# A written-out order of work with 73 places moved, and the last gate and value weights in one transfer each, in a kernel of two attentions and a gated feed-forward layer

## The chip, the cores and the metric

The kernel runs on one core of one Trainium2 chip. A core has a matrix engine (TensorE, in profiles PE; its weight loads are shown apart as PEld), a vector engine (VectorE, DVE), a scalar engine (ScalarE, ACT), a general engine (GpSimd, POOL) and a sync engine (SyncE, SP) which here only issues transfers. Each works through its own list of instructions in order and waits at semaphores for the others. Transfers between device memory (DRAM) and the core's SBUF run on 16 DMA engines beside them; PSUM is the small memory into which the matrix engine writes, eight banks of it.

The metric is the device time of one execution in microseconds (us).

## The reference, cut to what matters

Two attentions are computed per head and added: one over the sequence pooled by four, and one in which a position sees only the positions less than four away. The sum, with the heads laid side by side, goes through a feed-forward layer with a gate.

```python
batch, n_heads, seq, head_dim = (8, 8, 576, 64)
n_tokens, d_model, d_ff = (4608, 512, 1536)

def _attn_ref(q, k, v):                      # factor = 4, Sd = 144
    q_d = q.reshape(B, H, Sd, factor, D).mean(axis=3)     # k_d, v_d likewise
    out_d = sm_attn(q_d, k_d, v_d)
    out_up = np.repeat(out_d, factor, axis=2)
    mask = np.abs(pos[:, None] - pos[None, :]) < factor
    scores = np.where(mask, scale * np.matmul(q, k.transpose(0, 1, 3, 2)), -1e9)
    ...
    return out_up + np.matmul(attn, v)

def _moe_ref(x, w_gate, w_val, w_out):
    gate = np.maximum(x @ w_gate, 0.0)
    val = x @ w_val
    return gate * val @ w_out
```

## The kernel before

**The attention** goes by pairs of heads, 32 of them, numbered p = 0 to 31; four pairs make one batch of 576 tokens. Each pair is a chain of named steps, and the pair's number ends the name:

- lq, lk (L1430) load q and k; from pair 4 on one transfer serves two pairs. cast (L1330) turns them to 16 bits. For pairs 0 to 3 the loads land in the still unused tile gT and the casts in the still unused tile wo_sb, which is why these names stand in the trace.
- T (L1456, and L1460 for pairs 0 to 3) transposes them on TensorE into PSUM, for pairs 0 to 7; from pair 8 on a transposing transfer dT does it. ev0 and ev1 (one ev from pair 8 on) copy the result to qkT, pl pools it into qkd (L1330 for pairs 0 to 3, L1507 afterwards).
- S (L1518 the band, L1530 the pooled part; in pairs 0 to 3 two steps Sl, with the mask at L1537, and Sd) makes the scores in PSUM.
- msk, mx, sub, exp, sm, rc, nrm are the softmax of the band; nrm (L1615) multiplies by the reciprocal; tr0 and tr1 (L1621) transpose on VectorE.
- dmx, nb, exd0 to exd2 (L1605), rcd, nrd (L1631) are the softmax of the pooled scores. W (L1640) transposes them on TensorE and evw copies them out, for pairs 0 to 7; from pair 8 on a transfer dW does it.
- lv0 to lv3 (L1680) load v, vc (L1330) casts it. VP (L1695) and vd pool it (from pair 12 on l4, vs and vd).
- V (L1731, L1739) multiplies with v; od (L1750) scales the pooled part; xa0 and xa1 (L1759) add the two and write xT, the input of the feed-forward layer.

**The feed-forward layer** goes by blocks of tokens: 512 and 64 for the first batch and the second, then 512. For each of the 12 slices of d_ff (number j), hg and hv (L1798) multiply a block with a slice of the gate weights wg_sb and the value weights wv_sb, rl (L1812) is the ReLU and gm (L1819) the product into gT. hg0_6 is block 0, slice 6. hg512 and hg1088 are the small blocks of 64 tokens, six slices each. In the first block the slices 0 and 1 are split: hg0_0a works on three of the four parts of d_model, hg0_0b on the last, which comes from pair 3. y (L1864) multiplies 128 tokens of gT with wo_sb, yc (L1873) copies the result out and st stores it.

**The weights** come by transfers that GpSimd issues. The gate and value weights wg_sb and wv_sb come in four pieces each, 384 columns (three slices) a piece: wg0 to wg3 and wv0 to wv3, all at L1380; the output weights in four pieces wo0 to wo3 at L1385.

**What sets the order.** Every step is an Op with its engine (or several that could do it), its length as the author puts it, what it depends on, and a priority. A function list_schedule plans them all, with a model of the five engines, the transfers and the fetching of TensorE's instructions, and the result is one list of steps. A table RANKS of some 300 entries shifts priorities by name. The steps are then emitted in that order, and so each engine's list, the choice among engines, and the PSUM banks are fixed. Where the planner sees TensorE wait in the first 34 us of its plan, it fills the gap with matmuls of zeros (emit_zeros, L1360), 41 in all beside 12 at the very start (pewarm). Below, "a fill" is one such matmul.

Steps wait for one another by semaphores which the framework sets from the tiles that they read and write; SP's transfers also wait, each for the one eight places ahead of it.

## Time and profile before

| | us |
|---|---|
| median of 3 runs | 362.52 |
| lowest, highest | 361.52, 364.54 |
| the profiled execution, whole | 364.42 |
| its span, first to last instruction | 362.6 |
| busy: TensorE | 351.6 |
| busy: VectorE | 248.0 |
| busy: GpSimd | 204.7 |
| busy: ScalarE | 203.2 |

The span is what the views of the trace show; 1.8 us of the profiled execution's time lie around it. The mean granted clock of TensorE was 0.999.

How to read the rows: a row of the timeline has the start, the time, the engine, the line and operation, the tile written and those read, the size, how many alike were merged (x), and in square brackets how long the engine was idle before it and what released it. SPq is SP's queue of transfers. A row of windows has the stretch, its length, and for each engine the busy time and the count of instructions.

### The profile page before, as it was taken

Reading aid. Unit: us, or ns where it says so; the run is one execution under the profiler, and the core shown is the slowest. Engines: PE = TensorE matmul, PEld = TensorE weight load, DVE = VectorE, ACT = ScalarE, POOL = GpSimd, SP = SyncE. Lnnn points to the kernel's source line nnn. Section 1 sums busy time; section 2 is a strip of 40 time slices with the busy share of each in tenths; the row PEclk is TensorE's granted clock in tenths of the full one; section 3 lists DMA queues with packets and bytes.
Section 4 is the critical chain, followed back from the end, with each engine's and each line's share of the span. In section 5 each row is a group of like instructions: output and inputs, shape, how many; then the busy total and the mean of one; then the engine's idle time right before and its main releaser. Section 6 shows DMA issues by size and latency. Waiting matters only on the chain.

```text
span 362.6 us, 10503 instructions
## 1 busy us (share of the span) xinstructions
PE 351.6 (97%) x4241; PEld 182.4 (50%) x4241; DVE 248.0 (68%) x477; ACT 203.2 (56%) x481; POOL 204.7 (56%) x240
## 2 busy tenths in 40 slices
PE   8988998999999999999999999999999999999996
PEld 3545555445545554545545445444545454445554
DVE  4667997717988798978875986788979854222210
ACT  2477785627874857664566584767565533233222
POOL 7798573942477988674877468485899400000000
PEclk9999999999999999999999999999999999999999
DMA  7999999789999999999999999999996121011012
GB/s 185 190 260 258 195 188 302 124 181 165 283 225 215 219 275 167 254 225 250 196 220 243 164 303 156 215 282 174 238 236 101 40 77 47 0 60 59 0 72 105
DMA packets 122067, 64.80 MB, mean 179 GB/s; under 512 B 100386, under 2 KB 106402, under 8 KB 122018
## 3 DMA queue, kind: packets, MB, share of 16 engines
q1 hardware_dynamic: 116194, 59.41, 77.3%
q0 software_dynamic: 5824, 4.72, 8.5%
q8 instruction: 33, 0.54, 0.7%
q14 instruction: 16, 0.13, 0.1%
HBM read 47.59 MB, written 9.44 MB: 157 GB/s over the span
## 4 chain that ended last, share of the span: by engine, by line
PE 71%; DMA 13%; POOL 4%; SPq 4%; DVE 3%; issue 3%; ACT 1%; POOLq 0%; DVEq 0%; ACTq 0%
PE bank L1798 42%; PE bank L1864 20%; DMA qk<-in_q_dram 3%; DMA tq<-c 3%; PE bank L1518 2%; DMA v<-in_v_dram 2%; DMA vw<-in_v_dram 2%; PE bank L1731 2%; POOL wd L1631 1%; DMA gT<-in_q_dram 1%; SPq L1430 1%; PE bank L1739 1%; DMA wT<-wd 1%; PE bank L1530 1%; DVE qkd L1507 1%
## 5 line engine op out<-in xcount | busy, mean ns | idle before, releaser
L1819 DVE TENSOR_TENSOR gT<-r,bank 128x512 f16<-128x512 f16 (+1 forms) x112 | 74.5, 666 | 62.5 <-PE bank L1798 59.2
L1798 PE MATMUL bank<-xT,wg_sb 128*128 128x512 f16 (+2 forms) x528 | 112.3, 341 | 0.0
L1798 PE MATMUL bank<-xT,wv_sb 128*128 128x512 f16 (+2 forms) x528 | 112.2, 341 | 0.0
L1812 ACT ACTIVATE r<-bank 128x512 f16<-128x512 f32 (+1 forms) x112 | 65.1, 582 | 67.6 <-PE bank L1798 63.2
L1864 PE MATMUL bank<-wo_sb,gT 128*128 128x512 f16 x420 | 96.7, 379 | 0.0
L1798 PEld LDWEIGHTS <-wg_sb 128*128 128x128 f16 x528 | 44.2, 98 | 45.5 <-issue 0.4
L1798 PEld LDWEIGHTS <-wv_sb 128*128 128x128 f16 x528 | 44.2, 98 | 44.7 <-issue 0.9
L1864 PEld LDWEIGHTS <-gT 128*128 128x128 f16 x420 | 39.8, 98 | 44.6 <-issue 0.4
L1873 ACT COPY y_sb<-bank 128x512 f32<-128x512 f32 x35 | 20.5, 585 | 50.5 <-PE bank L1864 48.0
L1330 POOL CAST vw<-vw 128x1536 f16<-128x1536 f32 x28 | 40.9, 1462 | 3.4 <-DMA vw<-in_v_dram 2.5
L1507 DVE TENSOR_REDUCE qkd<-qkT 128x288 f16<-128x1152 f16 x28 | 37.6, 1342 | 4.9 <-ACT qkT L1329 4.4
L1586 POOL TENSOR_TENSOR s_sb<-s_sb,mx 128x384 f32<-128x384 f32 x28 | 23.2, 831 | 27.8 <-DVE mx L1583 27.1
L1605 ACT ACTIVATE wd<-bank,nmb 128x144 f16<-128x144 f32 x96 | 35.6, 380 | 5.0 <-POOL nmb L1595 4.2
L1621 DVE STREAM_TRANSPOSE at<-e 64x384 f16<-64x384 f16 x64 | 36.4, 569 | 2.0 <-POOL e L1615 1.3
L1615 POOL TENSOR_TENSOR e<-e,rs 128x384 f16<-128x384 f16 x32 | 26.8, 840 | 14.4 <-DVE rs L1613 10.8
L1631 POOL TENSOR_TENSOR wd<-wd,rsd 128x432 f16<-128x432 f16 x32 | 29.0, 909 | 9.6 <-DVE rsd L1627 8.3
L1759 DVE TENSOR_TENSOR xT<-bank,od_sb 128x288 f16<-128x288 f32 (+2 forms) x68 | 26.7, 430 | 9.5 <-ACT od_sb L1750 9.4
L1329 ACT COPY qkT<-tq 128x1152 f16<-128x1152 f16 x21 | 25.3, 1205 | 3.8 <-DMA tq<-c 3.8
L1717 POOL TENSOR_TENSOR vs<-v 104x512 f32<-104x512 f32 x20 | 25.4, 1269 | 1.4 <-DMA v<-in_v_dram 1.1
L1518 PEld LDWEIGHTS <-qkT 64*32 64x32 f16 x1536 | 16.6, 90 | 11.8 <-issue 7.2
L1330 POOL CAST c<-qk 128x1152 f16<-128x1152 f32 x16 | 18.2, 1147 | 5.7 <-issue 3.3
L1518 PE MATMUL bank<-qkT 64*32 64x32 f16 x1536 | 20.2, 178 | 0.9 <-DVE xT L1759 0.7
(67 smaller groups left out, 357.6 us busy)
## 6 DMA issues: line engine op xcount, KB each, us to landing
vw<-in_v_dram SPq DMA_DIRECT2D x126, 96.0 KB, 4.8
out_dram<-y_sb SPq DMA_DIRECT2D x16, 512.0 KB, 4.2
qk<-in_q_dram SPq DMA_DIRECT2D x14, 576.0 KB, 7.1
qk<-in_k_dram SPq DMA_DIRECT2D x14, 576.0 KB, 6.9
v<-in_v_dram SPq DMA_DIRECT2D x10, 640.0 KB, 7.1
wv_sb<-in_moe_w_val_dram POOLq DMA_DIRECT2D x4, 384.0 KB, 10.3
wg_sb<-in_moe_w_gate_dram POOLq DMA_DIRECT2D x4, 384.0 KB, 10.0
wo_sb<-in_moe_w_out_dram POOLq DMA_DIRECT2D x4, 384.0 KB, 7.8
```

Source lines behind the costliest of these rows:

```text
L1330: return lambda o: engine[eng].tensor_copy(out=dst, in_=src(o))
L1507: nc.vector.tensor_reduce(out=qkd[S3].rearrange("p (x t) -> p x t", x=2), in_=qk_sums, axis=AX.X, op=ALU.add)
L1518: nc.tensor.matmul(out=scv[32 * c : 32 * c + 32, i, :], lhsT=cols(hh, q0 + step * 24 * blk, 32), rhs=cols(hh, k0 + step * (24 * blk - 3), 32),
L1605: exd.append(add(ACT, 0.37, lambda o, i=i: nc.scalar.activation(out=_sap(wd_, 0, 128, 256 * i + K0, kd_cols), in_=_sap(dview()[:, i, :], 0 ...
L1615: r["nrm"] = nrm = add_any(either(lambda o, e: e.tensor_tensor(out=e_, in0=e_, in1=bc12(rs[S3]), op=ALU.mult), (POOL, 0.84), (DVE, 0.5)), ...
L1621: tr.append(add(DVE, 0.575, lambda o, lo=lo: nc.vector.transpose(out=at2[S3][lo : lo + 64, :, lo // 2 : lo // 2 + 32], in_=e_[lo : lo + 64 ...
L1631: r["nrd"] = nrd = add_any(either(lambda o, e: e.tensor_tensor(out=_sap(wd_, 0, 128, K0, w3), in0=_sap(wd_, 0, 128, K0, w3), in1=_sap(rsd[ ...
L1759: nc.vector.tensor_tensor(out=xT[:, kk, (c1 + lo) % XR : (c1 + lo) % XR + hi - lo].rearrange("p (t f) -> p t f", f=4), in0=bank[V.banks[hf ...
L1798: nc.tensor.matmul(out=bank[(h or o).banks[0]][:, n * x : n * x + n], lhsT=w_sb[:, kk, bass.ts(jj, 128)], rhs=xT[:, kk, x_col(t0) : x_col( ...
L1812: rl = add(ACT, 0.17 + 0.00083 * n * m, lambda o: nc.scalar.activation(out=rt[:, 0 : n * m], in_=bank[f1.banks[0]][:, 0 : n * m], func=AF. ...
L1819: gm = add(DVE, 0.15 + 0.00104 * n * m, lambda o: nc.vector.tensor_tensor(out=gT[:, js[0] : js[0] + m, pos : pos + n], in0=rt[:, 0 : n * m ...
L1864: nc.tensor.matmul(out=bank[parts[0].banks[0]], lhsT=gT[:, jj, col : col + 128], rhs=wo_sb[:, jj, :], start=(jj == 0), stop=(jj == NJJ - 1))
```

## The change

The planner, its constants, its model of transfers and of instruction fetch, and the table RANKS go. In their place stands ORDER, a text of 1771 words in the order of emission. A word is the name of a step, then, where needed, `.` with the PSUM banks, `:` with the engine (A, D, P), and `+n@b` with n fills into bank b ahead of it. Beside that the last two pieces of the gate weights become one (wg2, slices 6 to 11, 768 columns), and those of the value weights too (wv2).

```diff
-RANKS = {
...
-def list_schedule(ops, bank_pools, eps):
...
+ORDER = """
+zero3 zero8 lk0 zero5 zero7 warm pewarm.0 lq0 zero10 ld_id zero9 lk1 lq1 zero11 zero21 zero22
...
+lv3_5 tr1_3 hg0_0a.0+3@5 cast5:A lv2_4 tr0_3 wv1 hv0_0a.3 lv0_4 wg2 cast4:A VP3.6 lv1_4 T5.57 wv2
...
-    for g in range(4):
+    for g in range(3):
         for nm, dst, src in (("g", wg_sb, moe_w_gate), ("v", wv_sb, moe_w_val)):
-            w_ld[nm, g] = add(POOL, 0.85, wpiece(dst, src, 384 * g, 384), prio=-40 + g,
-                              xfer=2.55, after=W_AT[g], name=f"w{nm}{g}", port=(POOL,))
+            w_ld[nm, g] = add(POOL, 0.85, wpiece(dst, src, 384 * g, 384 if g < 2 else 768),
+                              prio=-40 + g, xfer=2.55 if g < 2 else 3.4, after=W_AT[g],
+                              name=f"w{nm}{g}", port=(POOL,))
...
-                    + [w_ld[nm, jj // 3] for jj in js], prio=FP + len(ops) + 10 * i,
+                    + [w_ld[nm, min(jj // 3, 2)] for jj in js], prio=FP + len(ops) + 10 * i,
...
-    order = list_schedule(ops, {"F": [0, 1, 2, 3], "A": [4, 5, 6, 7]},
-                          {PE: 0.05, ACT: 0.05, DVE: 0.05, POOL: 0.05, SP: 0.05})
...
+        for word in ORDER.split():
+            word, _, fill = word.partition("+")
+            word, _, banks = word.partition(".")
+            name, _, eng = word.partition(":")
+            o = named.pop(name)
+            o.banks = [int(b) for b in banks]
+            emit = next(f for e, _, f in o.alts if not eng or e == engines[eng])
+            if fill:
+                n, _, b = fill.partition("@")
+                emit_zeros(int(b), int(n))
+            emit(o)
```

The other numbers that the diff changes (the lengths 0.65, 0.45, 0.67, 0.34, 0.4 and 0.7 of some steps, the list called behind) were read by the planner alone and reach no instruction now.

Name by name, the two lists differ in the first two batches and the first steps of the third (pair 8's VP8 and ev8, and the load lk12), and are the same behind them. By engine:

- GpSimd loses nrm1, nrd0 and nrd1 to VectorE and the issues of wg3 and wv3; it takes cast7 from ScalarE. nb0 moves ahead of wg0, vc6 ahead of nb7, wo3 ahead of nrm6, nrd7 ahead of sub7.
- VectorE takes those three and also pl3, vd2 and ev1_4 from ScalarE; mx1 moves ahead of dmx0, sm0 ahead of dmx1, xa0_0 ahead of rc3, xa0_2 ahead of xa1_1, dmx7 behind xa1_5, rc6 ahead of gm0_9, gm0_10 behind pair 6's transposes, xa0_6 ahead of rc7.
- ScalarE has ev0_2 and ev0_3 two or three steps earlier, od1 behind exd2_3, exd0_6 ahead of rl512_6, ev8 ahead of yc2.
- TensorE has W2 ahead of Sd3, V3 ahead of hv0_1a, S4 behind hv512_0, S7 behind hv0_9 (and so W6 behind hg0_10), y2_0 ahead of VP7, y3_1 behind y1_2, VP8 ahead of hg576_1; and 49 fills where there were 41: T0 7 (5), T1 3 (8), T2 5 (3), Sl2 12 (10), Sd2 2 (0), T3 3 (3), W1 3 (4), V0 1 (0), V2 4 (6), W3 4 (1), hg0_0a 3 (1), T4 2 (0), the old numbers in brackets.
- SP has lk0 ahead of lq0, lq1 ahead of lv3_0, lq2 at place 8 where it stood at 12, and a few later transfers one to three places along.

GpSimd, from nb1 to wg1, about 16 to 30 us in the trace. Here s and e are the band's softmax (nrm is L1615, in the new file L619), wd the pooled one (nrd is L1631, new L635), `wo_sb<-gT` is cast3, vw a cast of v, nmb nb. Before:

```order
L1595 TENSOR_SCALAR nmb1_130<-nmx1_127 128x3
L1615 TENSOR_TENSOR e160_92<-e160_92,rs0_123 128x384
L1615 TENSOR_TENSOR e161_93<-e161_93,rs1_124 128x384
L1330 CAST vw160_84<-vw320_64 128x1536
L1330 CAST vw161_85<-vw321_65 128x1536
L1330 CAST wo_sb_70<-gT_76 96x2x12x64
L1595 TENSOR_SCALAR nmb2_131<-nmx2_128 128x3
L1631 TENSOR_TENSOR wd0_99<-wd0_99,rsd0_135 128x6x3x24
L1615 TENSOR_TENSOR e162_94<-e162_94,rs2_125 128x384
L1631 TENSOR_TENSOR wd1_100<-wd1_100,rsd1_136 128x6x3x24
L1631 TENSOR_TENSOR wd2_101<-wd2_101,rsd2_137 128x6x3x24
L1330 CAST vw162_86<-vw322_66 128x1536
```

The same stretch of GpSimd in the changed kernel:

```order
L599 TENSOR_SCALAR nmb1_130<-nmx1_127 128x3
L619 TENSOR_TENSOR e160_92<-e160_92,rs0_123 128x384
L332 CAST vw160_84<-vw320_64 128x1536
L332 CAST vw161_85<-vw321_65 128x1536
L332 CAST wo_sb_70<-gT_76 96x2x12x64
L599 TENSOR_SCALAR nmb2_131<-nmx2_128 128x3
L619 TENSOR_TENSOR e162_94<-e162_94,rs2_125 128x384
L635 TENSOR_TENSOR wd2_101<-wd2_101,rsd2_137 128x6x3x24
L332 CAST vw162_86<-vw322_66 128x1536
```

Three multiplies have left the stretch, one ahead of cast3 and two behind it.

VectorE, from sm2 on, in the changed kernel. The two rows of L635 are nrd0 and nrd1, the cast to qkd is pl3; in the kernel before none of these three stood here:

```order
L615 TENSOR_REDUCE sm2_122<-e162_94 128x12
L617 RECIPROCAL rs2_125<-sm2_122 128x12
L635 TENSOR_TENSOR wd0_99<-wd0_99,rsd0_135 128x6x3x24
L635 TENSOR_TENSOR wd1_100<-wd1_100,rsd1_136 128x6x3x24
L332 CAST qkd0_109<-bank4_142 128x288
L631 RECIPROCAL rsd2_137<-smd2_134 128x6
L625 STREAM_TRANSPOSE at22_89<-e162_94 64x12x32 x2
```

They stand ahead of rcd2 (`rsd2`), which followed the reciprocal `rs2` at once before.

VectorE where it waits for S7, about 62 us. `nmx1<-bank7` is dmx7, the first to read S7's scores. Before:

```order
L1592 TENSOR_REDUCE nmx1_127<-bank7_145 128x3
L1759 TENSOR_TENSOR xT_75<-bank6_144,od_sb1_113 128x288
L1611 TENSOR_REDUCE sm0_120<-e160_92 128x12
L1819 TENSOR_TENSOR gT_76<-r13_80,bank2_140 128x512
L1613 RECIPROCAL rs0_123<-sm0_120 128x12
L1580 TENSOR_TENSOR s_sb1_91<-bank5_143,mask_sb_73 128x384
```

The same stretch in the changed kernel:

```order
L596 TENSOR_REDUCE nmx1_127<-bank7_145 128x3
L615 TENSOR_REDUCE sm0_120<-e160_92 128x12
L617 RECIPROCAL rs0_123<-sm0_120 128x12
L823 TENSOR_TENSOR gT_76<-r13_80,bank2_140 128x512
L584 TENSOR_TENSOR s_sb1_91<-bank5_143,mask_sb_73 128x384
```

The addition to xT (xa1_5) now stands ahead of dmx7, and the reciprocal (rc6) ahead of the product (gm0_9). On TensorE S7 itself stood between hv0_8 and hg0_9 and stands now between hv0_9 and hg0_10.

1268 lines of the change are left out of this document (145 added, 1123 removed).

## The prediction, made before the changed kernel had run

> **What bounds the kernel now.** I read the busy times first, then every gap in TensorE's timeline, then the counts of its instructions by stretches.
>
> ```profile
> span 362.6 us, 10503 instructions
> PE 351.6 (97%) x4241; PEld 182.4 (50%) x4241; DVE 248.0 (68%) x477; ACT 203.2 (56%) x481; POOL 204.7 (56%) x240
> ```
>
> TensorE is busy for 97% of the span, so an edit pays only where TensorE waits, or is busy with fills. Its timeline shows where:
>
> ```profile
> 16.62 2.10 PE L1360 MATMUL bank<-r 128*128 128x512 f16 x9 [0.32 <-issue]
> ...
> 31.97 0.37 PE L1640 MATMUL bank<-ident_sb,wd 128*96 128x128 f16 x3 [0.36 <-POOL wd L1631]
> ...
> 32.71 0.33 PE L1640 MATMUL bank<-ident_sb,wd 128*96 128x128 f16 x3 [0.38 <-issue]
> ...
> 38.51 0.30 PE L1518 MATMUL bank<-qkT 64*32 64x32 f16 x20 [0.66 <-DVE xT L1759]
> ...
> 62.02 0.24 PE L1530 MATMUL bank<-qkd 64*32 64x144 f16 x2 [1.32 <-issue]
> ...
> 186.21 0.24 PE L1530 MATMUL bank<-qkd 64*32 64x144 f16 x4 [0.51 <-DVE qkd L1507]
> ...
> 228.12 0.41 PE L1739 MATMUL bank<-wT,vdz 104*128 104x144 f16 x4 [0.55 <-DMA wT<-wd]
> ```
>
> The rows of 31.97 and 32.71 are W3, behind which the feed-forward matmuls begin; that of 38.51 is S5, behind which hg0_0b stands. From there on TensorE stops only three times before the tail, at 62.02, 186.21 and 228.12. So the change has two places to win: the road to hg0_0b, and the 1.32 us inside S7. That wait, and those at 16.62 and 32.71, name no releaser. Counting TensorE's instructions up to each gap says what they are:
>
> ```profile
> 0.00:16.40 16.40, 14.68 (x223) 1.00 0.92 191
> 16.40:32.50 16.10, 13.28 (x256) 1.00 1.16 263
> 32.50:61.50 29.00, 27.26 (x512) 1.00 1.21 217
> ...
> 0.00:26.40 26.40, 22.66 (x353) 1.00 1.02 207
> 0.00:56.10 56.10, 50.63 (x867) 1.00 1.12 215
> ```
>
> The three gaps stand at matmul 223, 479 and 991: exactly 256 and 512 matmuls apart. I take them for waits for the next piece of the program, 128 matmuls with their weight loads, requested when TensorE enters the piece before. Matmul 351 was passed at about 26.4 and 479 came at 32.71, 6.3 us later; 863 was passed at about 56.0 and 991 came at 62.02, 6.0 us later. A piece that is worked off faster than in 6.0 to 6.3 us ends in a wait.
>
> By the Trainium skill (Runtime: NRT & Kernel Launch, Instruction fetch mechanics) instructions come in blocks of 256, fetched while the block before runs, and the cost of a boundary is "mostly hidden". The trace agrees with the block (128 matmuls and 128 weight loads) and shows the wait uncovered at three of the first eight boundaries. By that page alone the gap in S7 would have another cause and stay; that is rival 1.
>
> **S7 moved behind hv0_9.** The eight more fills shift every boundary eight matmuls earlier in the work, and S7 moves. Matmul 863 is now in W5 (its fifth of six) and 991 in S7 (its 31st of 60).
>
> ```profile
> 55.83 0.86 PE L1798 MATMUL bank<-xT,wg_sb 128*128 128x64 f16 x24
> ...
> 60.15 0.24 PE L1518 MATMUL bank<-qkT 64*32 64x32 f16 x10
> ...
> 62.21 1.04 PE L1798 MATMUL bank<-xT,wg_sb 128*128 128x512 f16 x4
> ...
> 63.95 0.50 PE L1640 MATMUL bank<-ident_sb,wd 128*96 128x128 f16 x6
> ```
>
> Between those boundaries lie now the end of W5 (0.1), hg512_6 to hv0_8 (60.15 - 55.83 = 4.3), hg0_9 and hv0_9 (63.95 - 62.21 = 1.7), and half of S7 (0.3): 6.4 us, where there were 4.7 (56.0 to 60.7). That covers a fetch of 6.0 to 6.3 us. Gain 1.3; the bounds are 0 (the wait reappears elsewhere) and 1.32.
>
> **The first pairs.** TensorE's work before hg0_0b hangs on the load of pair 3:
>
> ```profile
> 15.40 0.58 SPq L1430 DMA_DIRECT2D gT<-in_k_dram  x1
> ...
> 21.50 1.46 POOL L1330 CAST wo_sb<-gT 96x1536 f16<-96x1536 f32 x1 [0.31 <-DMA gT<-in_k_dram]
> ...
> 23.14 0.91 POOL L1631 TENSOR_TENSOR wd<-wd,rsd 128x432 f16<-128x432 f16 x1
> ...
> 24.28 0.40 ACT L1329 CAST qkd<-bank 128x288 f16<-128x288 f32 x1
> 24.56 1.21 ACT L1329 COPY qkT<-bank 128x576 f16<-128x576 f16 x2
> ...
> 24.43 0.19 DVE L1627 RECIPROCAL rsd<-smd 128x6 f32<-128x6 f32 x1 [1.77 <-ACT wd L1605]
> ...
> 13.23 0.56 DVE L1576 TENSOR_TENSOR s_sb<-bank,mx 128x384 f32<-128x384 f32 x1
> ```
>
> cast3 waits for lk3. SP issues lk3 in the same place with the same transfers ahead of it, so I leave cast3 at 21.5: all that the change wins earlier (lq2 four places sooner, nrm1 off GpSimd) ends in a longer wait there, and T3 stays at 23.0. Behind it things move. nrd0 and nrd1, 0.91 each on GpSimd, go to VectorE, which idles 1.77 us before rcd2; I price them by the nearest VectorE row at 0.56 each or little more, 1.2 together, which fits into that gap. So W1 no longer waits for nrd1. pl3 leaves ScalarE: ev1_3 ends 0.28 sooner (24.56 - 24.28), at 25.5 (24.56 + 1.21 - 0.28). The mask's matmul of Sl3 needs no ev1_3 and goes ahead; the rest of Sl3 begins at 25.6, where it began at about 26.4.
>
> Now the fetch takes over: 351 is Sl3's second matmul, passed at 25.6, so 479 comes at 25.6 + 6.3 = 31.9. It is the fourth fill before W3; that fill (2.10/9 = 0.23) and W3 (0.37) end at 31.9 + 0.6 = 32.5, where W3 ended at 33.04. Gain 0.5. Without the fetch the upper bound is what leaves GpSimd between cast3 and nrd3, which W3 waits for: 2 x 0.91 = 1.8. The lower bound is a loss of 0.6: nrd0 and nrd1 now run while GpSimd casts q and k of pair 3, and if the two engines exclude one another, cast3 ends up to 1.1 us late. No row of before shows VectorE with two operands from SBUF beside GpSimd; the nearest (13.23, one operand from PSUM) has the length that such a size needs, so I take no loss.
>
> By the Trainium skill (GPSIMD Engine Reference, Key points) the two engines share SBUF interfaces and contend when a VectorE instruction has two SBUF inputs; nrd0, nrd1 and nrm1 are such. By it the sum of this part would be -0.6 in place of +0.5; rival 2.
>
> The gain passes on. Behind W3 ScalarE's list is unchanged and without a gap:
>
> ```profile
> 33.08 0.63 ACT L1329 COPY wT<-bank 96x576 f16<-96x576 f16 x1 [1.31 <-PE bank L1640]
> 33.61 2.21 ACT L1329 CAST c<-qk 128x1152 f16<-128x1152 f32 x2
> 35.72 0.37 ACT L1329 CAST vdz<-bank 96x256 f16<-96x256 f32 x1
> 35.98 0.72 ACT L1329 COPY qkT<-bank 128x512 f16<-128x512 f16 x1
> ...
> 37.18 0.67 PE L1456 MATMUL bank<-ident_sb,c 128*128 128x128 f16 x9
> ...
> 36.74 1.35 DVE L1507 TENSOR_REDUCE qkd<-qkT 128x288 f16<-128x1152 f16 x1 [0.60 <-ACT qkT L1329]
> ...
> 38.01 0.81 DVE L1759 TENSOR_TENSOR xT<-bank,od_sb 128x288 f16<-128x288 f32 x2
> ```
>
> evw3, two casts, vd3, ev1_5, then pl5 and xa0_3 on VectorE: that chain releases S5 at 38.51, and hg0_0b follows. It starts 0.5 sooner. TensorE's own list from W3's end to T4's took 4.8 (33.04 to 37.85); V3 now stands ahead of hv0_1a, and four fills more (0.9) make it 5.7, 32.5 to 38.2, so it arrives with the chain (38.0) and takes no more than 0.2 of it. The 0.66 wait before S5 is filled, not won.
>
> **The weights.** wg2 and wv2 now carry two pieces each.
>
> ```profile
> 34.81 0.76 POOL L1380 DMA_DIRECT2D wv_sb<-in_moe_w_val_dram  x1
> ...
> DMA to landing us min/median/max: 12.3/12.3/12.3
> ...
> 36.27 0.78 POOL L1380 DMA_DIRECT2D wv_sb<-in_moe_w_val_dram  x1
> ...
> DMA to landing us min/median/max: 16.4/16.4/16.4
> ...
> 42.61 0.83 POOL L1586 TENSOR_TENSOR s_sb<-s_sb,mx 128x384 f32<-128x384 f32 x1 [4.40 <-DVE mx L1583]
> ...
> 52.44 1.03 PE L1798 MATMUL bank<-xT,wv_sb 128*128 128x512 f16 x4
> ```
>
> Two issues fewer (0.76 + 0.78) free GpSimd before cast6, which is not on the path; cast7 (about 1.2) goes into the 4.40 us that GpSimd idles before 42.61. Both cost nothing, and without that idle time at most 1.2. But slice 6 of the values, which landed at 47.1 (34.81 + 12.3), now comes with slices 9 to 11, which landed at 52.7 (36.27 + 16.4). hv0_6 needs it at 52.44 - 0.5 = 51.9. At an unchanged rate it would wait up to 0.8; but GpSimd's steps before those issues wait for Sl3's scores, 0.8 sooner (26.4 to 25.6), which covers that. I take nothing; bounds 0 and 0.8.
>
> **The rest.** Eight fills at 0.23 are 1.8 us of TensorE, all ahead of S5, where TensorE waits: nothing, or 1.8 if that cover went. S4 moves behind hv0_3, hg512_0 and hv512_0, 2.3 us of work; its first reader dmx4 stands in VectorE's list behind pl6 and gm0_3 and hardly moves. The moves from 64 us on change the order of work that TensorE does without a gap: nothing. The waits at 186 and 228 move along:
>
> ```profile
> 88.06 0.83 POOL L1586 TENSOR_TENSOR s_sb<-s_sb,mx 128x384 f32<-128x384 f32 x1 [7.97 <-DVE mx L1583]
> ```
>
> GpSimd idles 7.97 us until S8's scores are there, so the later pipeline starts from TensorE's time and shifts with it.
>
> **Sum.** 1.3 (S7) + 0.5 (first pairs) = 1.8. The span would be 362.6 - 1.8 = 360.8, the profiled execution 364.42 - 1.8 = 362.6. That execution was 1.9 above the median of the three runs, so against the median: 362.52 - 1.8 = 360.7 us.
>
> **Rivals.**
> 1. The gap in S7 is no fetch, or comes back at another boundary. For it: it names no releaser. Against it: 223, 479 and 991. Only 0.5 is left: 362.0.
> 2. VectorE and GpSimd hold each other up at cast3. For it: nrd0 and nrd1 fall on cast3. Against it: nothing measured. 1.3 - 0.6 = 0.7: 361.8.
> 3. Slower: the double transfer. The pieces landed (52.7 - 47.1)/2 = 2.8 us apart. If 768 columns run slower than two pieces, hv0_6 decides. wv1 landed at about 47.1 - 2 x 2.8 = 41.5; four more at 3.1 end at 53.9, 1.4 behind the 52.44 of before, which eats the 1.3 of S7; at 3.5 they end at 55.5, 3.1 behind, and the time is 362.5 + 3.1 - 1.3 = 364.3. Against it: the same bytes in fewer rows.
> 4. More: the fetch is quicker in this order or lk3 lands sooner, so the first pairs give up to 1.8: 362.5 - 3.1 = 359.4.
> 5. The moves are hidden and the wait in S7 only changes place: no change, 362.5.
>
> **Chances.** Forecast 0.45, rival 1 0.15, rival 2 0.13, rival 3 0.07, rival 4 0.12, rival 5 0.08. The runs of before spread over 3.0 us, so a single case reaches about 1 us to either side. The range goes from rival 4 less 1.0 to rival 5 plus 1.1: 358.4 to 363.6; rival 3 stays outside. A change within 1% (3.6 us) is about what a measurement of this kernel can't tell from none. Faster than 358.9 is half of rival 4 and a little of the forecast: 0.12. Slower than 366.1 is rival 3's far end and what I have not seen: 0.06. Within: 0.82.
>
> **What would show it.** Right: no idle time before L1530 near 60 us; cast3 still released by the load near 21.5; S5 and hg0_0b half a microsecond sooner; hv0_6 without a wait for a transfer; every later row shifted by 1.3 to 2.3. Wrong: a gap without a releaser at another boundary 128 matmuls along (rival 1 or 5); cast3 longer than 1.46 or nrd0 waiting (rival 2); TensorE idle before hv0_6 near 51 with a transfer as releaser (rival 3); or the waits near 186 and 228 growing by what was won before.

## The result, and the profile after

| | before | changed |
|---|---|---|
| median, us | 362.58 (13 runs) | 365.80 (13 runs) |
| lowest, highest | 361.52, 364.54 | 362.47, 369.58 |
| the profiled execution, whole | 364.42 | 366.69 |
| its span | 362.6 | 364.9 |

The changed kernel is slower: the ratio is 1.0073, 95% interval [1.0046, 1.01]. The forecast was 360.7 us and a range up to 363.6. The ratios here and below leave out runs more than 1.5% above a kernel's fastest (one of the changed kernel's 13, five of the twelve of sp_back, one of mid_fills_b), while the medians keep every run.

The head of the changed kernel's page: the span, busy times, and the clock granted to TensorE in 40 slices of 9.1 us. Below it is the row of the clock before.

```profile
span 364.9 us, 10513 instructions
PE 354.2 (97%) x4249; PEld 184.7 (51%) x4249; DVE 250.1 (69%) x483; ACT 201.3 (55%) x477; POOL 202.2 (55%) x236
PEclk9987999999999999999999999999999999999999
```

```profile
PEclk9999999999999999999999999999999999999999
```

TensorE is as full as before, 97%, but in the third and fourth slice, 18 to 36 us, the digits 8 and 7 say that its clock is below 90% of full speed; before, all are 9. Its timeline has the reason there (all gaps over 0.15 us between 15 and 140 us; the row of 20.18 is the work ahead of the long one):

```profile
15.82 2.32 PE L363 MATMUL bank<-r 128*128 128x512 f16 x10 [0.19 <-issue]
20.18 0.82 PE L363 MATMUL bank<-r 128*128 128x512 f16 x3
25.64 1.14 PE L460 MATMUL bank<-ident_sb,wo_sb 96*128 96x96 f16 x12 [4.64 <-POOL wo_sb L332]
...
137.33 0.82 PE L802 MATMUL bank<-xT,wv_sb 128*128 128x512 f16 x3 [0.56 <-issue]
```

The row of 25.64 is T3, the transposes of pair 3. Before, its row was this:

```profile
23.02 0.68 PE L1456 MATMUL bank<-ident_sb,wo_sb 96*128 96x96 f16 x12 [0.63 <-POOL wo_sb L1330]
```

TensorE now stands 4.64 us idle ahead of T3 where it stood 0.63, and T3 starts at 25.64, not at 23.02. There is no gap in S7 any more, none before S5 and none before hv0_6; a new one without a releaser stands at 137.33. T3 waits for cast3. GpSimd's timeline, in which `wo_sb<-gT` is cast2 and then cast3, and the rows of L383 are wv0 and wg0:

```profile
11.67 1.46 POOL L332 CAST wo_sb<-gT 96x1536 f16<-96x1536 f32 x1 [1.92 <-DMA gT<-in_k_dram]
13.08 0.97 POOL L383 DMA_DIRECT2D wv_sb<-in_moe_w_val_dram  x1
14.17 0.27 POOL L599 TENSOR_SCALAR nmb<-nmx 128x3 f32<-128x3 f32 x1
14.37 0.82 POOL L383 DMA_DIRECT2D wg_sb<-in_moe_w_gate_dram  x1
15.55 0.22 POOL L599 TENSOR_SCALAR nmb<-nmx 128x3 f32<-128x3 f32 x1 [0.36 <-DVE nmx L596]
15.75 0.82 POOL L619 TENSOR_TENSOR e<-e,rs 128x384 f16<-128x384 f16 x1
16.53 3.19 POOL L332 CAST vw<-vw 128x1536 f16<-128x1536 f32 x2
24.12 1.46 POOL L332 CAST wo_sb<-gT 96x1536 f16<-96x1536 f32 x1 [4.39 <-DMA gT<-in_k_dram]
```

cast3 itself waits 4.39 us for lk3, the load of pair 3. That load is issued by SP half a microsecond sooner than before (15.40), but lands 9.1 us behind its issue instead of 6.0. Its row in SP's queue in the changed kernel:

```profile
14.90 0.58 SPq L434 DMA_DIRECT2D gT<-in_k_dram  x1
```

The transfers of that stretch (KB each, us from issue to landing), the changed kernel's first, then those of before:

```profile
wv_sb<-in_moe_w_val_dram POOLq DMA_DIRECT2D x1, 384.0 KB, 6.9
wg_sb<-in_moe_w_gate_dram POOLq DMA_DIRECT2D x1, 384.0 KB, 10.4
...
gT<-in_k_dram SPq DMA_DIRECT2D x1, 288.0 KB, 9.1
```

```profile
wv_sb<-in_moe_w_val_dram POOLq DMA_DIRECT2D x1, 384.0 KB, 5.9
wg_sb<-in_moe_w_gate_dram POOLq DMA_DIRECT2D x1, 384.0 KB, 9.1
gT<-in_k_dram SPq DMA_DIRECT2D x1, 288.0 KB, 6.0
```

What went ahead of it is in the two lists. GpSimd issues wv0 and wg0 close behind cast2. Before, these rows of GpSimd stood later (the first is cast2):

```profile
13.03 1.46 POOL L1330 CAST wo_sb<-gT 96x1536 f16<-96x1536 f32 x1 [2.42 <-DMA gT<-in_q_dram]
14.44 0.97 POOL L1380 DMA_DIRECT2D wv_sb<-in_moe_w_val_dram  x1
15.40 0.75 POOL L1380 DMA_DIRECT2D wg_sb<-in_moe_w_gate_dram  x1
```

cast2 waited there for lq2, and the two issues stood beside lk3's at 15.40. Now lq2 comes four places sooner in SP's queue, cast2 begins at 11.67, and the two weight transfers are issued at 13.08 and 14.37, both ahead of lk3. In the 4.0 us behind lk3's issue GpSimd's queue moved 0.43 MB and SP's queue 0.22; before, it was 0.38 and 0.34. Theory W, as the experiments call it: these 768 KB take the DMA engines, lk3 lands late, and TensorE stands.

The stretches of two microseconds show what came on top (the column behind the five engines is the granted clock):

```profile
22.00:24.00 2.00, 0.00 (x0) 0.00 (x0) 0.93 (x2) 0.00 (x0) 0.00 (x0) 1.00 1.35 207
24.00:26.00 2.00, 0.36 (x5) 0.36 (x6) 0.00 (x0) 0.18 (x1) 1.88 (x3) 0.56 0.91 273
26.00:28.00 2.00, 2.00 (x27) 2.00 (x26) 0.22 (x1) 1.90 (x8) 0.59 (x1) 0.50 0.91 222
28.00:30.00 2.00, 2.00 (x13) 1.23 (x12) 1.35 (x4) 0.93 (x2) 1.52 (x2) 0.50 1.08 317
30.00:32.00 2.00, 2.00 (x71) 1.27 (x70) 0.78 (x2) 1.02 (x2) 0.79 (x1) 0.73 1.04 362
```

After the idle time the clock is granted at half rate. Each stretch's share below full speed, doubled, times its 2 us, gives 1.76 + 2 + 2 + 1.08 = 6.8 us at half clock, until about 31 us; the twelve transposes of T3's first half take 1.14 us where they took 0.68. It is no exception: the mean granted clock of its 13 runs is 0.990 to 0.995 (a stretch of 3.4 us at half clock makes 0.995 of a run of 363 us), and of the 129 runs of before that were measured beside the experiments, 114 have 0.999 or 1.0.

To see where the difference is made and won back, I took the start of some steps in TensorE's list, each found by counting matmuls (us from the start of the span):

| step | before | changed | difference |
|---|---|---|---|
| T3 | 23.02 | 25.64 | +2.62 |
| Sl3 | 26.13 | 30.09 | +3.96 |
| hg0_0b | 39.30 | 42.85 | +3.55 |
| hg0_6 | 51.24 | 54.79 | +3.55 |
| hg0_11 | 66.01 | 68.06 | +2.05 |
| hg1152_0 | 124.69 | 126.75 | +2.06 |
| y35_1, near the end | 358.13 | 360.40 | +2.27 |

2.6 us by the late load, 1.3 more while the clock is low; 0.4 and then 1.5 are won back, the second around S7; 0.2 goes again. The 1.3 is against the old order: from T3 to Sl3 took 3.11 us before and 4.45 now, but the new order takes 2.34 there at full clock (run warm below), so the low clock itself costs 2.1 us up to Sl3. Before's profiled execution was 1.8 above its median, the changed one's 0.9, hence 2.3 between the profiles and 3.2 between the medians.

### The profile page after: what moved, and what is told of

It is laid out like the page before. It is cut to its first block, busy times and chain, and to the rows that moved or that the text cites. A ratio compares the mean times of both kernels' runs of the same rounds, so it can differ in the third digit from the quotient of the medians.

```text
span 364.9 us, 10513 instructions
## 1 busy us (share of the span) xinstructions
PE 354.2 (97%) x4249; PEld 184.7 (51%) x4249; DVE 250.1 (69%) x483; ACT 201.3 (55%) x477; POOL 202.2 (55%) x236
## 4 chain that ended last, share of the span: by engine, by line
PE 77%; DMA 12%; SPq 4%; issue 3%; POOL 2%; DVE 2%; ACT 0%; POOLq 0%; DVEq 0%
PE bank L802 44%; PE bank L868 22%; DMA vw<-in_v_dram 3%; PE bank L522 3%; DMA qk<-in_q_dram 3%; DMA wT<-wd 3%; DMA gT<-in_k_dram 2%; PE bank L735 2%; PE bank L743 2%; SPq L684 1%; PE bank L534 1%; SPq L434 1%; PE bank L699 1%; POOL wd L635 1%; DVE vw L354 1%
## 5 line engine op out<-in xcount | busy, mean ns | idle before, releaser
L877 ACT COPY y_sb<-bank 128x512 f32<-128x512 f32 x35 | 20.5, 586 | 50.2 <-PE bank L868 47.8
L619 POOL TENSOR_TENSOR e<-e,rs 128x384 f16<-128x384 f16 x31 | 26.0, 839 | 14.3 <-DVE rs L617 10.3
L635 POOL TENSOR_TENSOR wd<-wd,rsd 128x432 f16<-128x432 f16 x30 | 27.3, 909 | 11.0 <-DVE rsd L631 9.9
L332 POOL CAST c<-qk 128x1152 f16<-128x1152 f32 x17 | 19.3, 1146 | 8.3 <-issue 2.6
L596 DVE TENSOR_REDUCE nmx<-bank 128x3 f32<-128x432 f32 x32 | 18.9, 594 | 3.2 <-PE bank L522 2.9
```

Source lines behind the costliest of these rows:

```text
L332: return lambda o: engine[eng].tensor_copy(out=dst, in_=src(o))
L619: r["nrm"] = nrm = add_any(either(lambda o, e: e.tensor_tensor(out=e_, in0=e_, in1=bc12(rs[S3]), op=ALU.mult), (POOL, 0.84), (DVE, 0.5)), ...
L635: r["nrd"] = nrd = add_any(either(lambda o, e: e.tensor_tensor(out=_sap(wd_, 0, 128, K0, w3), in0=_sap(wd_, 0, 128, K0, w3), in1=_sap(rsd[ ...
```

## The experiments

All start from the changed kernel unless said otherwise; the diffs show words of ORDER. Times are medians in us with lowest, highest and count; the ratio is to before, run on the same chip (its medians there: 362.3 to 362.8).

| run | median (lowest to highest, runs) | ratio, 95% interval |
|---|---|---|
| changed | 365.80 (362.47 to 369.58, 13) | 1.0073 [1.0046, 1.01] |
| w_late | 362.64 (361.50 to 365.60, 12) | 1.0012 [0.9989, 1.0036] |
| b_sp | 365.89 (364.33 to 368.86, 6) | 1.0106 [1.0065, 1.0147] |
| warm | 364.69 (362.81 to 367.24, 10) | 1.0061 [1.003, 1.0091] |
| w_late_s7 | 363.61 (362.11 to 365.26, 12) | 1.0035 [1.0012, 1.0057] |
| w_late_four | 363.38 (361.89 to 367.31, 12) | 1.0032 [1.0004, 1.0061] |
| mid | 362.31 (359.68 to 364.88, 12) | 0.9999 [0.9972, 1.0026] |
| mid_fills | 360.06 (359.10 to 362.76, 10) | 0.995 [0.9923, 0.9977] |
| mid_fills_b | 361.04 (359.91 to 365.99, 12) | 0.9974 [0.9947, 1.0002] |
| w_late_fills | 362.40 (361.03 to 363.77, 12) | 1.0 [0.9981, 1.0019] |
| w_late_pool | 363.56 (361.66 to 367.04, 12) | 1.0024 [0.9997, 1.0051] |
| sp_back | 365.28 (360.55 to 367.60, 12) | 1.0002 [0.9964, 1.0039] |
| sp_back_mid | 361.91 (360.23 to 364.26, 12) | 0.9983 [0.9956, 1.001] |
| sp_back_nrm1 | 362.32 (360.97 to 363.93, 12) | 1.0001 [0.998, 1.0022] |
| nrm1_pool | 364.74 (362.31 to 366.54, 12) | 1.0057 [1.0032, 1.0082] |

### The weights out of the way: w_late

```diff
- ... lv3_2 wv0 mx1 ... nb0 wg0 sm0 ... vc1:P Sl2.1+12@5
+ ... lv3_2 mx1 ... nb0 sm0 ... vc1:P wv0 wg0 Sl2.1+12@5
```

> The changed kernel with wv0 and wg0 moved on GpSimd from behind cast2 and nb0 to behind vc1 (issued near 18.5 and 19.5 us in place of 13.1 and 14.4); all else as in the changed kernel. Theory W (lk3 lands 9.1 us after its issue in place of 6.0 because the two weight transfers now start ahead of it and hold the DMA engines): lk3 lands before 21, cast3 starts by 20.5 (24.12 in the changed kernel), TensorE has no wait of over 1.5 us ahead of T3 and keeps its full clock there; 359 to 361.5 us against 365.8. Rival S (the new order of SP's own transfers, lq2 ahead of lv3_0 and lk2, makes lk3 late): cast3 still starts near 24, time within 1 us of 365.8.

362.64 against 365.80. w_late's timeline, cast3 and T3, and then the landing of its load:

```profile
21.44 1.48 POOL L332 CAST wo_sb<-gT 96x1536 f16<-96x1536 f32 x1
...
22.98 0.68 PE L460 MATMUL bank<-ident_sb,wo_sb 96*128 96x96 f16 x12 [1.71 <-POOL wo_sb L332]
```

```profile
gT<-in_k_dram SPq DMA_DIRECT2D x1, 288.0 KB, 4.2
```

The load lands 4.2 us behind its issue, cast3 no longer waits for it, and in this execution the clock stays full. In the 4.0 us behind the issue SP's queue moves 0.73 MB and GpSimd's none. The two words are worth 3.2 us, the whole loss between the medians. GpSimd's own list is no faster for it: nrm0 starts at 15.79, in the changed kernel at 15.75. The expectation wanted more: cast3 by 20.5, a wait of at most 1.5 us ahead of T3, and 361.5 us. The two issues now stand ahead of cast3 on GpSimd (wg0's at 20.70, 0.7 long), so it starts at 21.44.

### SP's order alone, in the kernel before: b_sp

The words of before, with only SP's first 17 transfers in the order of the changed kernel.

```diff
- lq0 lk0 ld_id lk1 lv3_0 lq1 lv2_2 lk2 ld_mask ld_sums lv0_1 lq2 ...
+ lk0 lq0 ld_id lk1 lq1 lv2_2 ld_mask lq2 lv3_0 lk2 lv2_1 ld_sums ...
```

> The kernel before with one part of the change alone: SP's first transfers in the order of the changed kernel (lk0, lq0, ld_id, lk1, lq1, lv2_2, ld_mask, lq2, lv3_0, lk2, ...); all other instructions as before. It brings cast2, and with it wv0 and wg0 directly behind cast2, about 1.3 us forward. Theory W (weight transfers issued ahead of lk3 make it late): wv0 issued near 13.1 and wg0 near 14.1, both ahead of lk3 near 14.9; lk3 takes 8 us or more to land, cast3 starts at 23 or later, TensorE's clock drops between 20 and 30 us; slower than before by 2 to 4 us. Rival (the collision needs the rest of the changed order): cast3 within 0.7 us of 21.5 and the time within 1 us of 362.6.

365.89: this part alone makes the kernel before as slow as the changed one. The timeline of b_sp, GpSimd and then TensorE at T3, and below it the stretch of ten microseconds:

```profile
11.61 1.47 POOL L350 CAST wo_sb<-gT 96x1536 f16<-96x1536 f32 x1 [2.00 <-DMA gT<-in_k_dram]
13.02 0.97 POOL L401 DMA_DIRECT2D wv_sb<-in_moe_w_val_dram  x1
13.99 0.76 POOL L401 DMA_DIRECT2D wg_sb<-in_moe_w_gate_dram  x1
...
22.27 1.47 POOL L350 CAST wo_sb<-gT 96x1536 f16<-96x1536 f32 x1 [1.88 <-DMA gT<-in_k_dram]
...
23.79 0.68 PE L478 MATMUL bank<-ident_sb,wo_sb 96*128 96x96 f16 x12 [2.20 <-POOL wo_sb L350]
```

```profile
20.00:30.00 10.00, 7.36 (x135) 4.80 (x137) 4.06 (x9) 4.97 (x14) 6.87 (x8) 0.83 1.13 290
```

The same chain: cast2 sooner, both weights issued ahead of lk3 (14.47 here, landing 7.7 us later), cast3 waiting, the clock below full. That profile is of a run at 364.35, near the lowest of the six, and there the load took a little less than the 8 us and cast3 started a little before the 23 us that were expected.

### A second profile of each kernel: before2 and after_p

> The kernel before, unchanged, for a second profile: the first profiled execution (364.42 us) stood 1.9 us above the median. If its waits are typical: 1.3 us in S7, 0.66 ahead of S5, cast3 near 21.5, within 0.3 us each. If that execution was an unlucky draw: one or more of these is shorter by 0.5 us or more and the span is 360 to 361.5.

> The changed kernel once more, for a second profile. If the late load is the rule, cast3 is released by it at 22.5 us or later, over 1 us behind the end of the casts vc0 and vc1 and T3 waits 2 us or more. If nrm1's hold-up is the rule, the multiply takes 3 us or more beside those casts, and the load is not what T3 waits for.

before2 ran in 362.64, with a wait of 1.04 inside S7 and 0.67 before S5; cast3 began at 21.12. The waits are typical, then, though the one in S7 is 0.3 shorter. It reached hg0_10 at 63.52, where the first profile of before did at 64.28, and the end 1.8 sooner: so much differs between two executions of one kernel.

after_p ran in 364.69. Its rows of cast3 and T3:

```profile
22.79 1.47 POOL L332 CAST wo_sb<-gT 96x1536 f16<-96x1536 f32 x1 [3.20 <-DMA gT<-in_k_dram]
...
24.31 0.68 PE L460 MATMUL bank<-ident_sb,wo_sb 96*128 96x96 f16 x12 [3.30 <-POOL wo_sb L332]
```

The late load again, 1.3 us less late, and half clock from 25.70 to 29.11.

### SP's order put back: sp_back, sp_back_p1, sp_back_p2, sp_back_mid, sp_back_nrm1

sp_back is b_sp the other way round: the changed kernel, with SP's first transfers in the order of before.

```diff
- lk0 lq0 ld_id lk1 lq1 lv2_2 ld_mask lq2 lv3_0 lk2 lv2_1 ld_sums ...
+ lq0 lk0 ld_id lk1 lv3_0 lq1 lv2_2 lk2 ld_mask ld_sums lv0_1 lq2 ...
```

> The changed kernel with SP's first transfers alone put back into the order of before; GpSimd's list, the fills, S7 and the joined weights stay as changed. If the loss is made by SP's new order alone, which lets cast2 and behind it wv0 and wg0 start ahead of the load of pair 3, cast2 begins near 13 us again, the load lands within 6.5 us of its issue, cast3 starts at 21.0 to 21.8, and the time is 361.5 to 363.0 us. If the other moves in the first batch (nrd0, nrd1 and nrm1 on VectorE, the fills) carry a share of the loss, it stays above 364.

This did not come out as theory W has it. Four of twelve runs lie at 360.6 to 362.3, eight at 364.5 to 367.6, so I go by the median and not by the ratio. The profile was of a run at 361.89: cast2 at 13.78, cast3 at 22.11 with a wait of 0.43, half clock from 11.83 to 15.24 and full clock behind that. Two more executions were profiled.

> sp_back once more, for its profile. If its runs of 364.5 us and more are the late load of pair 3, a profile of such a run shows cast3 released by that load at 23 us or later and T3 idle behind it for over 2 us; a run near 362 us shows cast3 at about 22.1, as the first profile did. If the slow runs have another cause, cast3 is at about 22 in a run of over 364.5 us, and the time is lost somewhere behind hg0_0b.

> The same kernel as sp_back_p1, a second draw, with the same two readings: over 364.5 us with cast3 at 23 us or later (the late load), or over 364.5 us with cast3 near 22 (another cause); a run near 362 tells nothing new.

sp_back_p1 (363.82) agrees with the first profile to 0.1 us from Sl3 (25.90 and 25.98) to hg1152_0 (122.66 and 122.61), and then loses 1.9 on the way to the end, so that part has nothing to do with the first batch. sp_back_p2 (365.66) shows something else. GpSimd, then VectorE, where nrm0 is the row of GpSimd at 16.25 and nrm1 that of VectorE at 16.65:

```profile
16.25 0.84 POOL L619 TENSOR_TENSOR e<-e,rs 128x384 f16<-128x384 f16 x1
17.03 2.87 POOL L332 CAST vw<-vw 128x1536 f16<-128x1536 f32 x2
```

```profile
16.65 3.67 DVE L619 TENSOR_TENSOR e<-e,rs 128x384 f16<-128x384 f16 x1
```

In the first profile of sp_back, which is the same program, the multiply takes its usual time, as in sp_back_p1 and in the changed kernel's first profile, whose row is the second here:

```profile
18.25 0.70 DVE L619 TENSOR_TENSOR e<-e,rs 128x384 f16<-128x384 f16 x1
```

```profile
16.29 0.70 DVE L619 TENSOR_TENSOR e<-e,rs 128x384 f16<-128x384 f16 x1
```

In sp_back_p2 and in the changed kernel, the multiply ends 0.42 us behind the GpSimd instruction that it waited for. In the changed kernel nrm0 ends at 15.75 + 0.82 = 16.57 and nrm1 at 16.29 + 0.70 = 16.99; there the casts behind nrm0 take 3.19 in place of 2.87. In sp_back_p2 the two casts end at 17.03 + 2.87 = 19.90 and nrm1 at 20.32. So when nrm0 ends, either VectorE goes next and the casts wait 0.3, or GpSimd keeps on and the multiply waits out both casts. The Trainium skill (SBUF — State Buffer, SBUF: two separate sides) calls the port pair of the two engines an exclusive lock, held for a whole instruction, which blocks a VectorE instruction with two SBUF inputs; these rows agree, and show the wait lasting over three GpSimd instructions in a row. In sp_back_p2 VectorE is behind for it, TensorE waits 1.97 us for nrd0 ahead of W0 (at 25.79), and hg0_0b starts at 40.10 against 38.74 in sp_back: 1.4 us. At nrm0 sp_back_p2 was still 1.5 us ahead (16.25 against 17.71), so between the two steps it lost 2.8.

> sp_back with the one multiply nrm1 back on GpSimd, behind nrm0 and ahead of vc0. If VectorE's multiply waiting out GpSimd's two casts makes the slow group of sp_back, that group goes: at most two of twelve runs above 364.5, median 361.8 to 363.3 us. If something else makes it, half or more of the runs stay above 364.5, as in sp_back (365.28).

```diff
- ... nrm1:D ...
+ ... nrm1:P ...
```

362.32, and no run above 363.93. The one multiply taken from VectorE makes the runs above 364 vanish. That each of those eight runs had the hold-up is not shown: sp_back_p2 is one execution, and its mean granted clock is 1.0, while the eight runs have 0.991 to 0.995, so each of them also had at least one stretch of half clock. Where it lay, and what the hold-up costs together with it, no profile shows.

> sp_back with wv0 behind nb0 and wg0 behind nrm0 in GpSimd's list, as in mid. If the weights ahead of the load of pair 3 make the slow runs of sp_back, the median is 361.5 to 363.0 us and at most two of twelve runs lie above 364.5. If something else of the change makes them, half or more of the runs stay above 364.5, as in sp_back.

```diff
- ... wv0 mx1 ... nb0 wg0 sm0 ... nrm0:P exd0_1
+ ... mx1 ... nb0 wv0 sm0 ... nrm0:P wg0 exd0_1
```

361.91, no run above 364.26. It doesn't tell the two causes apart: with wg0's issue between nrm0 and the casts, the multiply also finds the way free (0.70 in its profile).

### Is it nrm1 in the changed kernel too? nrm1_pool

The same one word, in the changed kernel itself.

```diff
- ... nrm1:D ...
+ ... nrm1:P ...
```

> The changed kernel with nrm1 alone back on GpSimd; SP's order and the weights stay as changed. If the late load of pair 3 is what most runs of the changed kernel pay for, the median stays at 364.8 to 366.3 us. If it is the hold-up of nrm1, the median falls to 362 to 363.5. If both have a share, it lies between, with the widest spread.

364.74, with the highest at 366.54. It lies just below the range for the late load, and the intervals of the ratios overlap with the changed kernel's. In its profile (of a run at 362.59) cast3 still waits 1.51 us for the load, T3 2.10, and the clock is 0.83 over 20 to 30 us. So the late load stays the main cause; a share of up to 1.1 us for the multiply isn't excluded.

### The clock: warm

23 fills in place of 3 ahead of T3, so that TensorE is busy until cast3 is there.

```diff
- T3.674+3@3
+ T3.674+23@3
```

> The changed kernel with 23 fills ahead of T3 in place of 3, which lengthens TensorE's work there by 20 x 0.22 = 4.3 us, about the 4.64 us that it waited. It tells the wait for lk3 from the slow clock behind the wait. If the slow clock costs time of its own (T3 1.9 us in place of 1.04, W0, W1 and Sl3 likewise, some 2 us in all): the clock stays 1.00 between 20 and 40 us, cast3 still starts near 24, and the time falls by 1 to 2 us, to 364 to 364.8. If the slow clock is hidden behind the softmax steps on the other engines: within 0.5 us of 365.8.

364.69, 1.1 below the changed kernel; the intervals overlap. Its clock is 1.00 over 20 to 30 us, but the fills end at 25.44, a microsecond behind cast3 (22.48 + 1.83 = 24.31), so it gives part of the gain away. The load itself also landed 1.6 us sooner in this execution than in the changed kernel's first profile. The starts of the steps show the price of the clock more plainly: the same steps from T3 to Sl3 take 4.45 us at half clock and 2.34 here (25.44 to 27.78).

### S7, the joined weights, the three multiplies: w_late_s7, w_late_four, w_late_pool

These take w_late, where the load isn't late, and undo one part each.

```diff
- hv0_8.1 lv1_8 ... hg0_9.3 ... vc6:P S7.57 hg0_10.0 dmx7 sm6 W6.4
+ hv0_8.1 S7.57 ... hg0_9.3 ... vc6:P W6.4 hg0_10.0 dmx7 sm6
```

> As the kernel with late wv0 and wg0, and S7 put back between hv0_8 and hg0_9 (and W6 ahead of hg0_10), as before the change. If the 1.32 us wait in S7 was a wait for the next 128 matmuls of the program: boundary 991 falls on S7's 39th matmul, about 4.8 us behind boundary 863, and TensorE waits there again, 1.0 to 1.4 us without a named releaser; 1.0 to 1.4 us over the kernel with late weights alone. If it was anything else that the rest of the change removed: no such wait and the same time within 0.4 us.

363.61, 1.0 above w_late, about as expected, though the intervals overlap. The wait inside S7 is back in its timeline:

```profile
60.83 0.20 PE L522 MATMUL bank<-qkT 64*32 64x32 f16 x4 [0.73 <-issue]
```

```diff
-    for g in range(3):
+    for g in range(4):
...
- ... VP3.6 lv1_4 T5.57 wv2 vd3:A
+ ... VP3.6 lv1_4 T5.57 wv2 wg3 wv3 vd3:A
```

> As the kernel with late wv0 and wg0, and the last two pieces of the gate and value weights as two transfers each again (wg2, wv2, wg3, wv3 of 384 columns, issued one behind the other where wg2 and wv2 stand). If the joined transfers are hidden either way, as no wait for them was seen in the changed kernel: the same time as with late weights alone, within 0.5 us. If the joined transfers shorten the busy time of the DMA engines enough to matter for the loads of q, k and v behind them: 0.5 to 1.5 us slower.

363.38 with four pieces of 384 columns again: 0.7 above w_late, in the range that was set for a gain by the joined transfers. But the intervals overlap widely, so this stays unclear; nothing shows the joined transfers to cost anything.

```diff
- ... nrm1:D ... nrd0:D ... nrd1:D ...
+ ... nrm1:P ... nrd0:P ... nrd1:P ...
```

> w_late with nrm1, nrd0 and nrd1 back on GpSimd. The prediction's step (three multiplies off GpSimd's path to nrd3 are worth 0.5 us, at most 1.8) says 363.1 to 364.4 us, with cast3 up to 0.9 later behind nrm1 and W1 waiting for nrd1. If VectorE's multiplies hold GpSimd up by as much as they take off it, the time stays within 0.4 us of w_late's 362.6, and nb2 and the casts beside them take their short times (0.23 and 1.46 us).

363.56 with nrm1, nrd0 and nrd1 on GpSimd again: 0.9 above w_late, the intervals overlapping. In its profile cast3 begins at 22.48 instead of 21.44, behind nrm1; 0.6 of this was there at nrm0 already (16.38 and 15.79). The three multiplies on VectorE thus seem to win something, but not all that GpSimd loses: w_late's row of nrd0 and nrd1, and the same of the changed kernel, where GpSimd stands idle beside them:

```profile
21.92 2.05 DVE L635 TENSOR_TENSOR wd<-wd,rsd 128x432 f16<-128x432 f16 x2
```

```profile
21.87 1.06 DVE L635 TENSOR_TENSOR wd<-wd,rsd 128x432 f16<-128x432 f16 x2
```

### A version that beats both: mid, mid_fills, mid_fills_b, w_late_fills

mid has the weights only as far back as they must go: wv0 behind nb0, wg0 behind nrm0.

```diff
- ... lv3_2 wv0 mx1 ... nb0 wg0 sm0 ... nb1 nrm0:P exd0_1
+ ... lv3_2 mx1 ... nb0 wv0 sm0 ... nb1 nrm0:P wg0 exd0_1
```

> The changed kernel with wv0 moved behind nb0 and wg0 behind nrm0 on GpSimd: issued near 14.4 and 16.6 us, so that one weight transfer starts ahead of lk3 (14.9) and the other behind it, as in the kernel before. Theory W: lk3 lands 4 to 6.5 us after its issue, by 21.4, cast3 starts by 21.5 with no slow clock; 360.5 to 362.5 us. If any weight transfer ahead of lk3 is too much: cast3 after 22.5 and over 363.5.

362.31, as fast as before. Its profile, of a run at 364.48, has cast3 at 21.96 with a wait of 1.35, and half clock from 24.75 to 28.16; nine of its twelve runs have a mean clock of 0.999 or 1.0. mid_fills takes eight of the 49 fills out besides.

```diff
- T0.456+7@1 ... Sl2.1+12@5 ... W3.4+4@4 ... T4.57+2@5
+ T0.456+5@1 ... Sl2.1+10@5 ... W3.4+2@4 ... T4.57
```

> As the last kernel, with 41 fills in place of 49 (T0 5, Sl2 10, W3 2, T4 0), so that the boundaries of 128 matmuls fall again as in the kernel before. In the changed kernel the boundary at matmul 2015 fell on hv1152_4 and showed a wait of 0.56 us at 137.33; with the old count it falls on hv1152_5. If these waits are set by the boundaries: no wait there, S7 still without one; faster than the last kernel by 0.3 to 1.0 us. If the waits come at whatever place: no difference beyond 0.3 us.

360.06, ratio 0.995 [0.9923, 0.9977]: faster than both kernels, with cast3 at 21.29 and hg0_0b at 38.05. TensorE's waits over 0.25 us between 15 and 140 us:

```profile
18.54 0.40 PE L699 MATMUL bank<-vw,sums_sb 128*32 128x256 f16 x6 [0.74 <-POOL vw L332]
...
22.82 0.68 PE L460 MATMUL bank<-ident_sb,wo_sb 96*128 96x96 f16 x12 [1.72 <-POOL wo_sb L332]
...
31.24 0.54 PE L644 MATMUL bank<-ident_sb,wd 128*96 128x128 f16 x6 [0.29 <-POOL wd L635]
...
133.98 0.82 PE L802 MATMUL bank<-xT,wv_sb 128*128 128x512 f16 x3 [0.27 <-issue]
```

The wait at the boundary of 128 matmuls, the row of 133.98, is 0.27 where mid's profile has 1.16 at 134.76. The boundary accounts for a part of the gain only: the expected gain was 0.3 to 1.0, the measured one is 2.25.

mid_fills_b takes only the last two of these four words (45 fills), w_late_fills puts all four into w_late.

> mid with fewer fills at W3 and T4 alone (45 fills; T0 and Sl2 keep theirs). These four stand where TensorE runs without a long wait behind W3: if the gain of mid_fills is theirs, the time is 360.0 to 361.0 us; if it came from T0 and Sl2, which stand ahead of the wait for cast3, or from the shifted boundaries of fetching, the time is 361.8 to 362.6, as mid.

> w_late with the fills of T0, Sl2, W3 and T4 as before (41 in place of 49). If the eight fills cost about 2 us in themselves, as they did between mid and mid_fills, this comes out at 360.0 to 361.2 us, faster than before. If what mid_fills won hung on the late load of pair 3 there, w_late_fills stays within 0.6 us of w_late, at 362.0 to 363.2.

mid_fills_b lies between: 361.04. But w_late_fills, with the same eight fills less, is no faster than w_late (362.40 and 362.64). So fewer fills are not simply worth their length, and why they pay in mid and not in w_late stays open. The clock is not the whole reason: among the runs with a mean clock of 0.999 or more the medians are 362.29 for mid (9 runs) and 360.06 for mid_fills (10), and 362.10 and 362.11 for w_late and w_late_fills (6 each). Nor do the profiles of mid and mid_fills point to nrm1, which takes 0.70 in both. Those two profiles are 4.3 us apart, 1.6 at hg1152_0 and 2.7 behind it, where mid waits 1.16 at 134.76 and 1.03 at 258.52 and mid_fills 0.27 and nothing.

## Why the prediction was wrong

The failed step is the one on the first pairs: "SP issues lk3 in the same place with the same transfers ahead of it, so I leave cast3 at 21.5: all that the change wins earlier (lq2 four places sooner, nrm1 off GpSimd) ends in a longer wait there". The place in SP's queue was the same, and lk3 was issued sooner. But the load shares the DMA engines with another queue, GpSimd's, and there wv0 and wg0 follow cast2. What the change won earlier did not end in a wait: it let 768 KB of weights go 1.0 to 1.4 us sooner, and cast3 began at 24.12. w_late (the weights moved away) and b_sp (this part alone) show it from both sides. It was worth 3.2 us between the medians. In the profiled execution T3 starts 2.6 us later for it, and the low clock behind the wait costs some 2.1 more.

- The gap in S7, 1.3 forecast: it went. The 128 matmuls ahead of it take 6.3 us now and took 4.7 before, as the prediction had it; with S7 put back the wait was back, 0.73 in its profile, and the median 1.0 higher. But the eight more fills moved the other boundaries too. The 128 matmuls ahead of matmul 2015 take 5.0 us now and took 6.7 before, and a wait without a releaser came there: 0.56 in the changed kernel's first profile, 1.03 at 135.31 in its second, none in either profile of before. That is rival 1, for which the sum had nothing.
- The rule of 6.0 to 6.3 us for such a piece does not hold: the 128 matmuls ahead of matmul 479 took 5.1 us in the changed kernel without a wait, and those ahead of matmul 1503 took 3.95 in the kernel before. What else must come together for a wait is open.
- The 0.5 forecast for the steps behind T3: in w_late, where T3 starts as before (22.98 and 23.02), Sl3 starts 0.8 sooner and hg0_0b 1.0 (38.29). The way was right and the size too small, in this one execution.
- nrd0 and nrd1 at 0.56 each on VectorE: 1.06 for both, right, as long as GpSimd stands idle. Beside cast3 they took 2.05. "I take no loss" was wrong: the engines exclude one another, as rival 2 had it. But it was mostly VectorE that waited, less so cast3 (1.48 in w_late, 1.83 in warm), and the worst of it was at a multiply that I had not priced, nrm1.
- hv0_6 without a wait: right. The joined weights at nothing: no run shows otherwise.
- Eight fills at nothing: no wait came of them where they stand, but they moved the boundaries. Taking them out of mid was worth 2.25 us, and out of w_late 0.2.
- None of the rivals had the weights of GpSimd's queue ahead of lk3. Rival 3, the slower one, had a late transfer, but the wrong one.

Without the failed step the forecast would not have come true either. w_late and mid, whose load is hardly late or not late at all, run at 362.64 and 362.31, as fast as before and not 1.8 faster. In the profiles the gain is there for a while: hg1152_0 starts at 122.17 in w_late and at 123.94 in before2. Behind it, where the two programs have the same steps, w_late loses 1.1 us again, with a wait of 1.03 for a transfer at 256.21. The prediction took the later waits to move along unchanged, and that did not hold. mid_fills, at 360.06, comes near the 360.7 of the forecast, but by way of the fills, which the forecast priced at nothing: that is luck.

## What to carry to other kernels

A load's landing can hang on another queue's transfers, as lk3's did here: when a change lets one queue run ahead, list what it issues in the same microseconds as the load that the bound engine waits for, and place bulk transfers that are needed late (the weights here, not used before 32 us) behind that load's issue by their position, not by luck. When a multiply with two SBUF operands is moved from GpSimd to VectorE, look at what stands on GpSimd beside it: it may wait for several instructions in a row. And a wait read from one execution is a draw; take a second profile before it is priced. Fills and other small insertions shift every later boundary of 128 matmuls: price the boundaries that they move, not only the one that is to go.
